# Attention: projection in 64-row halves beside the scores and exponents of the other half, attended values between such stretches

## The chip, the cores and the metric

The kernel runs on one core of a Trainium2 chip. The metric is device time in microseconds of one execution, the median of three runs. The core's engines work side by side, each through its own queue in order: TensorE (PE, with its weight loads listed as PEld), VectorE (DVE), ScalarE (ACT), GpSimd (POOL), and SyncE (SP), which only issues DMAs. TensorE multiplies on an array of 128 by 128 cells; a matmul that uses only 64 rows of its operands takes one half of the array, rows 0 to 63 or rows 64 to 127, and one that writes 32 partitions takes a column strip. Its results land in PSUM, eight banks of 512 numbers a partition, where VectorE and ScalarE read them.

## The reference

Two pairs of layers on x of 2048 tokens by 576 features. Each pair is windowed attention and then a spectral filter, both behind a layer norm and added to x:

```python
def _A_ref(x, wqkv, wo):            # H = 32 heads of 18, window W = 256
    q, k, v = (x @ wqkv), by head
    scores = einsum("bhqd,bhkd->bhqk", q, k) * 18 ** -0.5
    scores = where(0 <= q_index - k_index < 256, scores, -1e9)
    o = einsum("bhqk,bhkd->bhqd", softmax(scores), v)
    return o @ wo
def _B_ref(x, w_r, w_i):
    return irfft2(rfft2(x) * (w_r + 1j * w_i))
x = x + _A_ref(layernorm(x)); x = x + _B_ref(layernorm(x))     # and both once more
```

## The kernel before, in words

The change touches the middle of each attention layer, the function `layer_a`, which is run once for each of the two attention layers.

The layer first makes xh and xl, the normalised x transposed and split into a high and a low part, and v. Then q and k are made by **projection**: `proj(i, c)` (L787) makes 128 rows of the joint q and k (block i of 9) for 512 tokens (c of 4) in a PSUM tile pj, as 14 matmuls of 128 rows that add up (high by high, low by high, high by low; `k_steps` gives the order). I call one (i, c) a *unit*. When its last matmul is issued, ScalarE copies the high part of the tile to sg (L813), and a `remainder` is noted: VectorE makes the low part (L816) and a DMA stores both to qk_d (L818). `remainders()` runs what is noted. At the eighth matmul of c = 2 the weights of block i + 1 are split (L796).

The heads go in 8 groups of four. `stack_load` brings a group's rows from qk_d into the tiles qs and ks: two heads in rows 0 to 63 and two in rows 64 to 127, each as high and low slots stacked, so that one matmul of 64 rows gives a whole score. The two heads of a half are told apart by `pair`, the halves by `hp`.

A group has 16 blocks of 128 tokens, and x counts blocks over all groups, 0 to 127. For a block there are three things to do:

- `score_max(x, pair, hp)` (L844): a matmul S of 63 rows gives the scores of 128 queries against up to 384 keys, and VectorE takes their masked maximum (L859). After four blocks `m_rows` turns the maxima with a transpose tpm, ScalarE negates them to mt, and a DMA writes them to the 64th row of qs.
- `exps(x, pair, hp)` (L877): a matmul E of 64 rows gives the transposed scores less the maximum, and ScalarE writes their exponent to a tile P (L890). After the fourth one GpSimd clears what lies outside the window (L892, L895).
- `pv(x)` (L900): the attended values, eight matmuls with fp32 operands that add into the PSUM tile U. Four heads write four strips of 32 partitions. After four blocks ScalarE copies U to us (L914), and `norm` turns us with four transposes tpo and divides on VectorE.

The main loop (L955) counts a step t from -10 to 129. A step has scores for block t + 10, exponents for block t, attended values for block t - 2 and some matmuls of the projection. Its order on TensorE is: E of both halves, S of both halves, U, then E of both halves and S of both halves for the other pair, then the projection's matmuls, then at most one transposition (tpm or tpo) that is due. The matmuls of E come in pairs, rows 0 to 63 and then rows 64 to 127, and so do those of S. `goal` (L946 to L950) spreads the 22 units that remain at t = 2 over t = 2 to 102; a step in which a unit ends makes no transposition.

PSUM's eight banks: three for S (tpm and tpo too), three for E, one for pj, one for U. In the first units pj uses an E bank every other time; in the last steps half of the E use S banks.

The order on each engine is the order of the calls: nothing is rescheduled. After the loop come the output projection and the spectral filter, which the change touches only in the names of the banks they use first.

Of the kernel before, what the change touches and what calls it, by code (L numbers as in the profile page):

```python
# [8 lines left out]
F32 = mybir.dt.float32  # L9
# [6 lines left out]
S, D = 2048, 576  # L16
# [592 lines left out]
def layer_a(tc, ident, eps, bp, src, dst, wqk_d, wv_d, wo_d, dc_d, gc_d, dram, copy, wvs, second, spectral, share):  # L609
# [17 lines left out]
    if True:  # L627
# [134 lines left out]
        with ExitStack() as c2:  # L762
# [24 lines left out]
            def proj(i, c, bank=0):  # L787

                box = {}
                ks = k_steps()  # L790
                cs = slice(c * 512, c * 512 + 512)

                def mm(s, k):
                    wk, p, xk = k
                    if s == 7 and c == 2 and 0 < i < 8:
                        w_split(i + 1)  # L796
                    if s == 0:
                        box["ps"] = pp.tile([128, 512], F32, tag="E" if bank else "pj", name=f"pj{i}_{c}", bufs=3 if bank else 1)
                    w = wt[i][0] if p == "h" else wt[i][1]
                    x = tokens(xT(xk, slice(0, S)), c) if second else xT(xk, cs)  # L800
                    T.matmul(box["ps"].rearrange("r (n p) -> r n p", n=NT) if second else box["ps"], w[:, wk], x, start=s == 0, stop=s == len(ks) - 1)  # L801
                    if s == len(ks) - 1:
# [17 lines left out]
                return [lambda s=s, k=k: mm(s, k) for s, k in enumerate(ks)]  # L820
# [25 lines left out]
            def score_max(x, pair, hp):  # L846
# [4 lines left out]
                if t == hp == pair == 0:  # L851
                    ms[n, c] = wp.tile([128, 2, 2, 4], F32, tag="m", name=f"m{n}_{c}", bufs=3)
# [9 lines left out]
            def m_rows(n, c):  # L862
                q = qs[n % 2]
                tp = pp.tile([128, 4, 128], F32, tag="S" if t >= 0 else "E", name=f"tpm{n}_{c}", bufs=3)
# [10 lines left out]
            pt = {}  # L875

            def exps(x, pair, hp):  # L877
# [5 lines left out]
                if hp == pair == 0:  # L883
# [3 lines left out]
                ps = pp.tile([128, 512], F32, name=f"E{x}_{hl_}", **(dict(tag="S", bufs=3) if pair and NX - LEAD <= x < NX - 4 else dict(tag="E", bufs=3)))  # L887
# [3 lines left out]
                if hp == pair == 1:  # L891
# [39 lines left out]
            for k, (i, c) in enumerate(((0, 0), (1, 0), (0, 1), (1, 1), (0, 2), (0, 3), (1, 2), (1, 3))):  # L931
                for f in proj(i, c, k % 2):
                    f()
# [9 lines left out]
            pj = [f for i in range(2, 9) for c in range(4) for f in proj(i, c, c % 2 if i == 2 else c == 0 and i == 3)]  # L943
# [11 lines left out]
            for t in range(-LEAD, NX + 2):  # L955
# [29 lines left out]
                for f in more:  # L985
                    f()
                if t >= 1:
                    remainders()
# [109 lines left out]
```

## Time and profile before

| | |
|---|---|
| three runs | 1567.22, 1568.28, 1578.97 us, median 1568.28 |
| span of the profiled execution, first to last instruction | 1561.3 us |
| the median less that span | 7.0 us |
| TensorE busy | 1495.4 us, 96% of the span |
| weight loads | 1086.4 us, 70% |
| VectorE, ScalarE, GpSimd busy | 976.1, 806.4, 624.6 us |
| mean granted TensorE clock | 0.993 |

The page gives a span for the profiled execution and no other time of its own, so the 7.0 us are taken against the median. In a line of the profile the first word after the numbers is the engine, L801 is line 801 of the kernel, `pj<-xh,wqh` is the output and the inputs, `64*128 64x384` a matmul's weights and its moving operand. Ends of matmuls are modelled; starts are measured. In a row of the chain or of the waits the name behind the arrow is what ended the wait.

### The profile page before, as it was taken

To read this page: it belongs to the slowest core of one execution; us is meant where nothing else is said; L and a number is where in the kernel's file an instruction comes from. 1 tells how busy PE (TensorE), PEld (TensorE's weight loads), DVE (VectorE), ACT (ScalarE), POOL (GpSimd) and SP (SyncE) were. 2 spreads that over 40 slices of the span, in tenths; PEclk is the share of its full clock that TensorE was granted. 3 is DMA by queue.
4 is the path that set the end of the run, shared out by engine and by line. 5 is a ranking of instruction groups with operands and counts; after the bars stand their busy time and mean duration, and the time that the engine had idled before them with its cause. 6 is when DMAs were issued, how large, how long until landed. Compare 5 with 4: busy or idle time off the path is not lost.

```text
span 1561.3 us, 34502 instructions
## 1 busy us (share of the span) xinstructions
PE 1495.4 (96%) x12124; PEld 1086.4 (70%) x12124; DVE 976.1 (63%) x3152; ACT 806.4 (52%) x1900; POOL 624.6 (40%) x1026
## 2 busy tenths in 40 slices
PE   7999999999999899999999999999999998999998
PEld 7975555555555899858999755555555558998598
DVE  4327777777775555455852377777777755554577
ACT  5523666666667344323454246666666673442243
POOL 2172444444446233162321823443443563322434
PEclk9999999999999999999999999999999999999999
DMA  6656455555553456666764564555535543657664
GB/s 196 186 178 213 138 163 175 155 157 171 153 162 99 144 181 193 214 240 226 257 166 96 184 209 136 151 149 148 144 122 144 150 142 116 199 183 248 213 217 137
DMA packets 203130, 267.62 MB, mean 171 GB/s; under 512 B 103183, under 2 KB 108303, under 8 KB 201999
## 3 DMA queue, kind: packets, MB, share of 16 engines
q1 hardware_dynamic: 194638, 245.44, 51.8%
q10 hardware_dynamic: 7680, 15.59, 2.8%
q0 software_dynamic: 640, 4.39, 1.0%
q8 instruction: 97, 1.59, 0.4%
q14 instruction: 75, 0.61, 0.1%
HBM read 166.71 MB, written 102.00 MB: 172 GB/s over the span
## 4 chain that ended last, share of the span: by engine, by line
PE 70%; DVE 7%; DMA 6%; ACT 5%; POOL 5%; issue 1%; SPq 1%; POOLq 0%; DVEq 0%; ACTq 0%
PE pj L801 16%; PE U L909 11%; PE E L889 11%; PE S L857 7%; PE ops L555 6%; PE vps L738 4%; PE pf L202 3%; PE pz L215 3%; DMA ofree<-yd 2%; PE pi L361 2%; PE tpo L919 2%; ACT P L890 2%; PE po L382 2%; DVE ofree L298 1%; POOL uv L302 1%
## 5 line engine op out<-in xcount | busy, mean ns | idle before, releaser
L859 DVE CUSTOM_DVE_ANT_0 jk<-S,mask 128x384 bf16<-128x384 f32 (+2 forms) x1024 | 499.0, 529 | 148.8 <-PE S L857 146.0
L890 ACT ACTIVATE P<-E 128x384 f32<-128x384 f32 (+2 forms) x1024 | 423.2, 474 | 200.6 <-PE E L889 185.3
L892 POOL TENSOR_SCALAR_AFFINE_SELECT P<-P 128x512 f32<-128x512 f32 x256 | 163.0, 637 | 440.1 <-ACT P L890 438.0
L889 PE MATMUL E<-qs,ks 64*128 64x384 f32 (+2 forms) x1024 | 235.6, 429 | 12.4 <-ACT P L890 9.0
L857 PE MATMUL S<-ks,qs 63*128 63x384 f32 (+2 forms) x1024 | 212.3, 351 | 3.2 <-DVE m L859 2.4
L909 PE MATMUL U<-P,vq 128*19 128x128 f32 (+1 forms) x3840 | 204.9, 332 | 1.0 <-POOL P L895 1.0
L889 PEld LDWEIGHTS E<-qs,ks 64*128 64x128 f32 x1024 | 103.7, 184 | 145.3 <-ACT P L890 81.7
L909 PEld LDWEIGHTS U<-P,vq 128*19 128x19 f32 x3840 | 90.5, 98 | 101.3 <-issue 36.3
L801 PE MATMUL pj<-xh,wqh 128*128 128x512 f32 x360 | 158.0, 439 | 2.1 <-ACT vt L742 1.7
L895 POOL TENSOR_SCALAR_AFFINE_SELECT P<-P 128x512 f32<-128x512 f32 x224 | 142.6, 636 | 0.0
L857 PEld LDWEIGHTS S<-ks,qs 63*128 63x128 f32 x1024 | 116.5, 188 | 37.2 <-DVE m L859 27.1
L555 PE MATMUL ops<-oroom 128*128 128x288 f32 x840 | 120.8, 299 | 4.4 <-DVE oroom L538 3.0
L801 PE MATMUL pj<-xh,wql 128*128 128x512 f32 x360 | 122.9, 414 | 0.1
L801 PE MATMUL pj<-xl,wqh 128*128 128x512 f32 x288 | 120.9, 420 | 0.0
L555 PEld LDWEIGHTS ops<-oroom 128*128 128x128 f32 x840 | 112.8, 189 | 6.2 <-DVE oroom L538 4.0
L801 PEld LDWEIGHTS pj<-xh,wqh 128*128 128x128 f32 x360 | 68.0, 189 | 37.3 <-issue 24.2
L816 DVE TENSOR_TENSOR sg<-pj,sg 128x512 fp32r<-128x512 f32 x72 | 49.8, 691 | 61.8 <-ACT sg L813 61.8
L171 POOL TENSOR_TENSOR eo<-xn 128x287 f32<-128x287 f32 x32 | 26.1, 817 | 153.1 <-ACT xn L169 142.1
L859 DVE DVE_READ_ACCUMULATOR2_ANT m<- 128x1 f32 x1024 | 85.2, 83 | 0.0
L813 ACT CAST sg<-pj 128x512 fp32r<-128x512 f32 x72 | 42.4, 588 | 75.4 <-PE pj L801 73.8
L361 PE MATMUL pi<-oroom 128*128 128x256 f32 (+1 forms) x576 | 76.0, 285 | 5.4 <-ACT oroom L346 4.0
L801 PEld LDWEIGHTS pj<-xh,wql 128*128 128x128 f32 x360 | 64.7, 188 | 23.5 <-issue 13.5
(177 smaller groups left out, 2593.7 us busy)
## 6 DMA issues: line engine op xcount, KB each, us to landing
qk_d<-sg SPq DMA_DIRECT2D x56, 512.0 KB
qs<-qk_d SPq DMA_DIRECT2D x384, 72.0 KB
ks<-qk_d SPq DMA_DIRECT2D x384, 72.0 KB
v_d<-vt SPq DMA_DIRECT2D x32, 304.0 KB
vq<-v_d SPq DMA_DIRECT2D x16, 608.0 KB
yd<-ye SPq DMA_DIRECT2D x32, 290.0 KB
wt<-in_w SPq DMA_DIRECT2D x16, 580.0 KB
x<-ofree SPq DMA_DIRECT2D x32, 288.0 KB
```

What stands on the lines that cost most here:

```text
L361: T.matmul(o, z[:, sl, c, lo:lo + m], mo, start=k == 0, stop=k == 5)
L555: self.nc.tensor.matmul(self.ps[u][n][:, 0:288], x, self.w[p][:, wk * D + n * 288:wk * D + n * 288 + 288], start=first and i == 0, stop=la ...
L738: T.matmul(ps[:, n, 0:288], xT(xk, c), w[:, wk, n * 288:(n + 1) * 288], start=i == 0, stop=i == len(ks) - 1)
L801: T.matmul(box["ps"].rearrange("r (n p) -> r n p", n=NT) if second else box["ps"], w[:, wk], x, start=s == 0, stop=s == len(ks) - 1)
L816: V.tensor_sub(rest[:, 1], by, rest[:, 0].bitcast(F32))
L857: T.matmul(ps[:, 0:N], q[b:b + 63, pair, i * 128:i * 128 + 128], k[b:b + 63, pair, lo:hi], start=True, stop=True)
L859: V.tensor_tensor_reduce(out=jk[:, 0:N], in0=ps[:, 0:N], in1=mask[:, 384 - N:384], scale=1.0, scalar=-3e38, op0=ALU.add, op1=ALU.max, accu ...
L889: T.matmul(ps[:, 0:nq], k[b:b + 64, pair, j * 128:j * 128 + 128], q[b:b + 64, pair, j * 128:j * 128 + nq], start=True, stop=True)
L890: A.activation(p[:, hl_, 0:nq], ps[:, 0:nq], AF.Exp, scale=SC)
L892: P.affine_select(out=p[:, :, 0:128], in_=p[:, :, 0:128], pattern=[[0, 4], [1, 128]], compare_op=ALU.is_ge, fill=0.0, base=0, channel_mult ...
L895: P.affine_select(out=p[:, :, 256:384], in_=p[:, :, 256:384], pattern=[[0, 4], [-1, 128]], compare_op=ALU.is_gt, fill=0.0, base=0, channel ...
L909: T.matmul(U[32 * h:32 * h + 19, (q0 % 4) * 128:(q0 % 4) * 128 + 128 * (q1 - q0)], vts[n][:, j, h], pt[n, j][:, h, (q0 - j) * 128:(q1 - j) ...
```

## The change

The projection matmuls of the 22 units after t = 2 are cut into halves of 64 rows: a unit is 14 matmuls on the lower rows and 13 on the upper (the last product of low by low is left out), 27 in place of 14. They go beside E and S of the other half of the array.

A step of t = 2 to 102 becomes: `half` on one side, a drain of TensorE, `pv`, the transposition that is due, `half` on the other side. A `half` has four matmuls of one half of the array (E for two pairs, S for two pairs) and two or three projection matmuls of the other half, merged by a running sum of 176 for an E or S and 230 for a projection matmul. The side alternates so that the second `half` of a step and the first of the next are on the same side; in the first `half` of a step (at = 0) the order is S, E, S, E, in the second (at = 1) E, S, E, S.

The lower and the upper matmuls of a unit add to the same bank, at different times. The banks change: two for E (three before), two for pj (one before). From t = 103 the old order stays, and the second pair of E uses the banks of pj. A step in which a unit ends now makes its transposition as well. Which of the four exponents of a block comes first now varies, so the tiles P and m are made at the first and the masks at the fourth, whichever it is. The first six of the remaining units and the eight before them stay whole, all on the two pj banks.

```diff
-            def proj(i, c, bank=0):
+            def proj(i, c):
-                box = {}
-                ks = k_steps()
+                box = dict(n=0)
...
-                def mm(s, k):
+                def mm(r, k, of, cue):
                     wk, p, xk = k
-                    if s == 7 and c == 2 and 0 < i < 8:
+                    if cue and c == 2 and 0 < i < 8:
                         w_split(i + 1)
-                    if s == 0:
-                        box["ps"] = pp.tile([128, 512], F32, tag="E" if bank else "pj", name=f"pj{i}_{c}", bufs=3 if bank else 1)
+                    if box["n"] == 0:
+                        box["ps"] = pp.tile([128, 512], F32, tag="pj", name=f"pj{i}_{c}", bufs=2)
+                    box["n"] += 1
...
-                return [lambda s=s, k=k: mm(s, k) for s, k in enumerate(ks)]
+                ks = k_steps()
+                whole = [lambda s=s, k=k: mm(slice(0, 128), k, 14, s == 7) for s, k in enumerate(ks)]
+                lower = [lambda s=s, k=k: mm(slice(0, 64), k, 27, s == 7) for s, k in enumerate(ks)]
+                upper = [lambda k=k: mm(slice(64, 128), k, 27, False) for k in ks[:13]]
+                return whole, lower, upper
...
-                ps = pp.tile([128, 512], F32, name=f"E{x}_{hl_}", **(dict(tag="S", bufs=3) if pair and NX - LEAD <= x < NX - 4 else dict(tag="E", bufs=3)))
+                tag = "E" if x < MIX or not pair else "S" if NX - LEAD <= x < NX - 4 else "pj"
+                ps = pp.tile([128, 512], F32, name=f"E{x}_{hl_}", tag=tag, bufs=3 if tag == "S" else 2)
...
-            for m in range(22):
-                a, b = [2 + 23 * z // 5 for z in (m, m + 1)]
-                for t in range(a, b):
-                    goal[t] = 84 + 14 * m - (-14 * (t + 1 - a) // (b - a))
+            MIX = 103
+            units = [proj(i, c) for i in range(2, 9) for c in range(4)]
+            pj = [f for u in units[:6] for f in u[0]]
+            halves = [[f for u in units[6:] for f in u[side]] for side in (1, 2)]
+            def half(t, hp, at):
+                side = halves[1 - hp]
+                k = len(side) - (22 * (14 - 1 + hp)) * (MIX - 1 - t) // (MIX - 2)
+                steps = [(230 * z, z, f) for z, f in enumerate(side[:k])]
+                del side[:k]
+                ops = [(exps, t, 0), (score_max, t + LEAD, 0), (exps, t, 1), (score_max, t + LEAD, 1)]
+                if not at:
+                    ops = [ops[z] for z in (1, 0, 3, 2)]
+                steps += [(176 * z + 1, z, lambda f=f, x=x, pair=pair: f(x, pair, hp)) for z, (f, x, pair) in enumerate(ops)]
+                for _, _, f in sorted(steps, key=lambda z: z[:2]):
+                    f()
+                remainders()
...
+                mix = 2 <= t < MIX
...
+                if mix:
+                    half(t, 1 - t % 2, 0)
+                    T.drain()
+                    if 0 <= t - 2 < NX:
+                        pv(t - 2)
-                for pair in range(2):
+                for pair in range(0 if mix else 2):
...
                 for f, n, c in [] if ends and t >= 2 else due[:1]:
                     f(n, c)
                     due.pop(0)
+                if mix:
+                    half(t, t % 2, 1)
```

More of the change, by code (lines that the diff above doesn't have):

```diff
@@ L850, in score_max @@
                 q, k = qs[n % 2], ks_[n % 2]
-                if t == hp == pair == 0:
+                if (n, c) not in ms:
                     ms[n, c] = wp.tile([128, 2, 2, 4], F32, tag="m", name=f"m{n}_{c}", bufs=3)
@@ L873, in m_rows @@
                                           mt[r:r + 4].bitcast(F32))
-            pt = {}
+            pt, made = {}, {}
             def exps(x, pair, hp):
@@ L984, in layer_a @@
                         more = more[(len(more) + 1) // 2:]
[L985 to L988, printed above, removed]
+                if not mix:
+                    for f in more:
+                        f()
+                    if t >= 1:
+                        remainders()
                 if copy and t >= 32 and t % 4 == 0 and t < 32 + 16 * len(copy):
```

26 lines of the change are left out of this document (13 added, 13 removed).

## The prediction, made before the change was run

> **What bounds the kernel now.** I read the page from its busy shares to the chain that ended last, then cut out the stage that the change touches, then looked at one of its steps instruction by instruction.
>
> ```profile
> span 1561.3 us, 34502 instructions
> ...
> PE 1495.4 (96%) x12124; PEld 1086.4 (70%) x12124; DVE 976.1 (63%) x3152; ACT 806.4 (52%) x1900; POOL 624.6 (40%) x1026
> ...
> PE 70%; DVE 7%; DMA 6%; ACT 5%; POOL 5%; issue 1%; SPq 1%; POOLq 0%; DVEq 0%; ACTq 0%
> PE pj L801 16%; PE U L909 11%; PE E L889 11%; PE S L857 7%; PE ops L555 6%; PE vps L738 4%; PE pf L202 3%; PE pz L215 3%; DMA ofree<-yd 2%; PE pi L361 2%; PE tpo L919 2%; ACT P L890 2%; PE po L382 2%; DVE ofree L298 1%; POOL uv L302 1%
> ```
>
> TensorE is on 70% of the chain, and the four kinds of matmul that the change rearranges (projection pj, attended values U, exponent inputs E, scores S) hold 45% of the span. The table by stages, between the attended values of step 1 and of step 101 in each layer:
>
> ```profile
> 148.32:447.34 299.02, 295.78 (x2731) 165.15 (x2729) 223.66 (x869) 197.12 (x476) 129.75 (x208) 1.00 0.53 158
> 925.21:1224.69 299.48, 296.33 (x2731) 164.71 (x2729) 223.66 (x869) 197.21 (x476) 122.05 (x192) 1.00 0.50 143
> ```
>
> A hundred steps take 299 us, so one takes 2.99, in both layers and at a granted clock of 1.00 (the figure behind the five engines). The engines stand in the order TensorE, weight loads, VectorE, ScalarE, GpSimd: VectorE has 224 of the 299 us, ScalarE 197. So TensorE sets the step, and the next engine is a quarter below it. Inside a step, from the timeline (start, length as modelled; only the starts are used here):
>
> ```profile
> 312.92 0.45 PE L889 MATMUL E<-qs,ks 64*128 64x384 f32 x2
> 313.20 0.34 PE L857 MATMUL S<-ks,qs 63*128 63x384 f32 x2
> 313.47 0.85 PE L909 MATMUL U<-P,vq 128*19 128x256 f32 x16
> 314.25 0.44 PE L889 MATMUL E<-qs,ks 64*128 64x384 f32 x2
> 314.52 0.34 PE L857 MATMUL S<-ks,qs 63*128 63x384 f32 x2
> 314.80 0.50 PE L801 MATMUL pj<-xh,wqh 128*128 128x512 f32 x1
> 315.13 0.39 PE L801 MATMUL pj<-xl,wqh 128*128 128x512 f32 x1
> 315.36 0.40 PE L801 MATMUL pj<-xh,wqh 128*128 128x512 f32 x1
> 315.60 0.27 PE L865 MATMUL tpm<-ident,m 128*16 128x128 f32 x1
> 315.80 0.45 PE L889 MATMUL E<-qs,ks 64*128 64x384 f32 x2
> ...
> 318.72 0.60 PE L919 MATMUL tpo<-ident,us 128*128 128x128 f32 x4
> 319.25 0.45 PE L889 MATMUL E<-qs,ks 64*128 64x384 f32 x2
> ```
>
> What the reader should see: a pair of E or S, one matmul on each half of the array, starts together and costs the time of one; and every change of array layout costs. From pj to the next pj is 0.23, but the first pj after S needs 0.33: 0.10 is a weight load that nothing covers. E to S is 0.28, of which again about 0.10 is load, so a 384-wide pair streams in 0.17. S to pj or U is 0.27, which leaves 0.10 for the changeover itself. So a changeover costs 0.10, and 0.20 where full-width weights follow. A step has four: into U (0.10), out of U (0.20), into pj (0.20), out of pj (0.20), together 0.70. Streams: four pairs 0.68, U 0.78 less the 0.10 of its way out, 0.68, and 3.05 pj (22 units of 14 over 101 steps) at 0.23, 0.70. With the transposes (tpo 0.53 less the 0.10 changeover that pj would have had, once in four steps; tpm 0.10 net, once in four) 0.13. Sum 2.89; the other 0.10 is waiting.
>
> **The change part by part.** It acts on 101 steps a layer, 202 in all.
>
> Streams: nothing. A step after has eight E and S on one half, 8 x 0.17 = 1.36, beside 27 x 22 / 101 = 5.88 half-height pj on the other, 5.88 x 0.23 = 1.35. Before it was 0.68 + 0.70 = 1.38. The same columns pass; they are only paired otherwise.
>
> Does a pair out of step run as fast as one in step? The trace has a few such places, where one half had waited:
>
> ```profile
> 476.54 0.44 PE L889 MATMUL E<-qs,ks 64*128 64x384 f32 x1 [0.38 <-ACT P L890]
> 476.64 0.54 PE L857 MATMUL S<-ks,qs 63*128 63x384 f32 x2
> ...
> 485.59 0.34 PE L857 MATMUL S<-ks,qs 63*128 63x384 f32 x2
> 485.60 0.19 PEld L889 LDWEIGHTS E<-qs,ks 64*128 64x128 f32 x1
> 485.77 0.33 PE L889 MATMUL E<-qs,ks 64*128 64x384 f32 x1
> ```
>
> At 476.64 two S of the two halves overlap though they start 0.20 apart (0.54 for both, 0.34 for one), and at 485.60 a half loads its next weights while it streams: the next matmul starts after 0.18. So I take the halves as independent.
>
> Changeovers: into and out of pj go, **-0.40**. But the transposes lose their place beside pj: they now stand behind U, with a changeover and load of their own, 0.20, in two steps of four, **+0.10**.
>
> The drain: 202 of them, ahead of U. No row shows one in the middle of a kernel. It must wait until results have landed. E at 314.25 streams until 314.53, and its reader starts at 314.72:
>
> ```profile
> 314.72 0.87 ACT L890 ACTIVATE P<-E 128x384 f32<-128x384 f32 x2 [0.46 <-PE E L889]
> ...
> 485.79 0.87 ACT L890 ACTIVATE P<-E 128x384 f32<-128x384 f32 x2 [1.30 <-PE E L889]
> 486.33 0.18 PEld L889 LDWEIGHTS E<-qs,ks 64*128 64x128 f32 x1 [0.55 <-ACT P L890]
> ...
> L890 ACT ACTIVATE P<-E 128x384 f32<-128x384 f32 x352 | 153.2, 492 | 70.9 <-PE E L889 63.6 <-PE S L857 4.2 <-PE U L909 1.7
> ```
>
> That is 0.20, an estimate of the emptying. Restarting costs 0.05: the ACT that began at 485.79 ends 0.49 later, at 486.28, and the waiting load starts at 486.33. So 0.25 in place of the 0.10 of an ordinary changeover: **+0.15**. Below: nothing, if the changeover already empties the array. Above: the waits table has idle of U's weight loads put down to issue, at most 0.4 long.
>
> ```profile
> PEld E L889 <- ACT P L890: 32.5, 100, 0.7
> ...
> PEld U L909 <- issue: 13.9, 58, 0.4
> ```
>
> A drain with such a gap behind it costs 0.20 + 0.40 - 0.10 = 0.50. I take 0.15, the nearer row being that of a wait of this very stage. Behind the drain stand U's sixteen matmuls, a transpose and the next stretch; ACT and VectorE wait for that stretch, and have 1.0 and 0.7 us of a step to spare.
>
> The banks: E has two in place of three, pj two in place of one. Between two U a stretch now brings E S E S | S E S E on one half. By hand, from the start of the first load at 0: E1 streams 0.10 to 0.27, S1, then E2 0.44 to 0.61; unhindered, E3 would stream from 0.95 and E4 from 1.29, ending at 1.46. ACT reads E1 from 0.27 + 0.20 = 0.47 to 0.96, and its bank is free at 1.01. E3's load waits for that on TensorE's queue, with the pj steps behind it; E3 streams from 1.11, 0.16 late. ACT starts a second exponent 0.38 after the first (0.87 for the two), so E2's bank is free at 0.85 + 0.49 + 0.05 = 1.39. E4's load waits for it and streams from 1.49 to 1.66: the stretch is 0.20 longer. VectorE reads a score in 0.56:
>
> ```profile
> 300.40 0.56 DVE L859 CUSTOM_DVE_ANT_0 jk<-S,mask 128x384 bf16<-128x384 f32 x1 [0.17 <-PE S L857]
> ```
>
> It reads S1, streamed by 0.44, from 0.64 to 1.20, and its bank (one of three, as before) is free at 1.25, about when S4 loads; four reads and the little else that it has leave it at 2.24 a step. So **+0.20**, with nothing at the lower end, if ACT takes the exponents sooner than I reckon, and 0.34 at the upper, the second rival's.
>
> Other edits. The projection's stores, weight splits (same step, same unit) and loads keep their steps: a unit ends within a step of where it did, a head group's rows are loaded some four steps or more after the last unit they need, and scored ten steps later. Nothing on SP's or POOL's queue moves past anything that is late. POOL finishes a step's probabilities one step ahead of U. In the steps after 103 the second pair of E gets pj's two banks, four in all instead of three; the wait there is
>
> ```profile
> PEld E L889 <- ACT P L890: 8.5, 23, 0.7
> ```
>
> 8.5 us in layer 1, and I give back a quarter of it, 2 us a layer, -4.
>
> Sum per step: -0.40 + 0.10 + 0.15 + 0.20 = +0.05, and x 202 = +10; less 4, **+6 us**. Span 1561.3 becomes 1567. The runs' median, 1568.28, is 7.0 above the span of the profiled execution; the same lies around it after, so 1574.
>
> **The rivals.**
>
> Faster: *the drain is free.* If the 0.10 changeover is already an emptying of the array, the drain adds nothing: 1574 - 202 x 0.15 = 1544. For it: U's first load today follows the last S only after that gap. Against it: a reader needs 0.20, not 0.10, after the stream ends, and a drain waits like a reader.
>
> Slower: *ACT's other work falls into the stretch.* With two E banks every ScalarE instruction between E1 and E4 delays both halves at once, since they share one queue. By the same window,
>
> ```profile
> L914 ACT COPY us<-U 128x512 f32<-128x512 f32 x25 | 14.7, 587 | 1.2
> ...
> L813 ACT CAST sg<-pj 128x512 fp32r<-128x512 f32 x22 | 13.0, 590 | 2.4 <-PE pj L801 2.3
> ```
>
> they are 27.7 us per 100 steps, 0.28 a step; if half of it delays an exponent, +0.14 x 202 = +28: 1602. It decides from the point where they come behind E1 instead of beside U. The copy of U comes before E1 and should fit; the cast comes at any place of the stretch.
>
> Slower too: *one weight load at a time.* If a half can't load while the other does, the 14 loads of a stretch follow one another. At 0.10 to 0.11 each, as read from the starts, they take 1.40 to 1.54, where the streams take 1.36; I take +0.11, x 202 = +22: 1596. It decides from 1.36 / 14 = 0.097 for a load. Against it: a pair's two loads cost the 0.10 of one.
>
> *Matmuls must end in order.* A 384-wide E issued right behind a 512-wide pj would have to end 0.06 after its own time; the lane catches up within the stretch, so about +0.05 a step, +10: 1584. The trace has only pairs of equal width and can't tell. The Trainium skill (TensorE: Matmul & The Clock Gate, Part 3, "What overlaps and what doesn't") states that matmuls start and end in program order; by it this rival is the one that holds. The same place says that a weight load overlaps a running matmul only on other rows of the array; the row at 485.60 shows it on the same rows, and the measurement decides.
>
> *It doesn't do what it says:* halves of different kinds run one after the other. Then 1.36 + 1.35 in place of 1.36, +1.35 x 202 = +273: about 1850. Against it: the rows of 476.64.
>
> **How the numbers follow.** Forecast 1574: 0.40. Drain free, 1544: 0.25. ACT's other work, 1602: 0.18. One load at a time, 1596: 0.06. Ends in order, 1584: 0.07. Not side by side, 1850: 0.04. The forecast's own spread is some 15 us, from the bank wait (0.13 to 0.27 a step). Half of the first rival, with a shorter bank wait, lies below 1544, down to 1534 for most; the slow ones reach 1612 if ACT delays a little more than half: 1534 to 1612 leaves out the 1850, the dear drain (1574 + 202 x 0.35 = 1645, for which only the longest of 58 waits speaks) and the tails. A measurement of this kernel tells about 1% from no change, 15.7 us. Faster by over 1% (below 1553): most of the drain rival and a little of the forecast, 0.26. Slower (above 1584): the two slow mechanisms, half of the ends in order, the 1850, and the forecast's upper edge, 0.36. Within: 0.38.
>
> **What would show it.** In the profile after: E and pj starting together in the timeline, E to S 0.17 apart in a stretch; no 0.33 for a first pj; 0.25 between the end of a stretch and U's first load (0.10 if the drain is free, more than 0.3 if it is dear); the row of E's weight loads waiting for ACT at some 20 us more per 100 steps; VectorE's 224 us unchanged, at the same share of a step of 3.0 us. The prediction is wrong if the step is under 2.93 or over 3.07 us, and its reason is wrong if the drain and the banks don't carry it.

## The result, and the profile after

The changed kernel takes 1580.45 us (median of 20 runs, 1576.78 to 1586.00), the kernel before took 1570.75 us beside it (20 runs, 1562.67 to 1578.97). The ratio is 1.0063, with a 95% interval of 1.0047 to 1.0079: the change costs about 0.6%. The forecast was 1574. From profile to profile the span grew from 1561.3 to 1576.3 us, by 15.0, where 6 were forecast. The medians lie closer than the spans because of the clock: both profiled executions had a mean granted clock of 0.993, but the 52 executions of the kernel before that stand beside the experiments have 0.988 by median, and the 20 of the changed kernel 0.9925. Those with 0.992 or more take 1564.4 us (8 of the kernel before) and 1579.6 us (17 of the changed kernel) by median, so that at a like clock the change costs 15 us, 1.0%. Four lines of the page of the changed kernel answer to those shown of before (span, busy shares, and the chain by engine and by line):

```profile
span 1576.3 us, 35829 instructions
...
PE 1483.9 (94%) x12696; PEld 1127.6 (72%) x12696; DVE 964.6 (61%) x3152; ACT 810.6 (51%) x1900; POOL 622.8 (40%) x1026
...
PE 70%; DVE 7%; ACT 6%; DMA 4%; POOL 3%; issue 3%; SPq 1%; POOLq 0%; DVEq 0%; ACTq 0%
PE pj L801 15%; PE U L916 12%; PE E L895 7%; PE S L862 7%; PE ops L555 6%; PE vps L738 4%; PE pf L202 3%; PE pz L215 3%; PE tpo L926 2%; ACT P L896 2%; PE pi L361 2%; PE po L382 2%; ACT sg L813 1%; DMA yd<-ze 1%; PE pq L313 1%
```

TensorE still holds 70% of the chain, and its four kinds of matmul 41% of the span in place of 45%. What is new is "issue": 3% in place of 1%, time in which the engine waited for nothing that the profile shows. The same hundred steps, from the attended values of step 1 to those of step 101, in the table by stages of the changed kernel (length, then TensorE, weight loads, VectorE, ScalarE, GpSimd, granted clock):

```profile
146.88:453.91 307.03, 290.76 (x3010) 183.46 (x3010) 218.45 (x870) 200.00 (x479) 130.28 (x210) 1.00 0.52 157
931.17:1239.33 308.16, 291.97 (x3009) 183.98 (x3009) 218.02 (x868) 199.99 (x478) 122.07 (x193) 1.00 0.50 142
```

A step takes 3.070 and 3.082 us where it took 2.990 and 2.995: 8.0 and 8.7 us more per hundred, 16.7 in all, which is more than the 15.0 of the span (in the 25 steps behind them 61.9 and 59.3 us became 58.2 each, 4.8 us back; elsewhere 3.1 are lost). TensorE's busy time within a step fell, and VectorE and ScalarE have what they had. So TensorE waits where it did not wait before. One usual step of the changed kernel, in the timeline:

```profile
347.09 0.85 PE L916 MATMUL U<-P,vq 128*19 128x256 f32 x16
347.86 0.49 PE L801 MATMUL pj<-xl,wqh 64*128 64x512 f32 x1
347.87 0.44 PE L895 MATMUL E<-qs,ks 64*128 64x384 f32 x1
348.15 0.34 PE L862 MATMUL S<-ks,qs 63*128 63x384 f32 x1
348.20 0.39 PE L801 MATMUL pj<-xh,wqh 64*128 64x512 f32 x1
348.33 0.34 PE L895 MATMUL E<-qs,ks 64*128 64x384 f32 x1
348.43 0.39 PE L801 MATMUL pj<-xl,wqh 64*128 64x512 f32 x1
348.50 0.33 PE L862 MATMUL S<-ks,qs 63*128 63x384 f32 x1
348.66 0.39 PE L801 MATMUL pj<-xh,wql 64*128 64x512 f32 x1
348.68 0.33 PE L862 MATMUL S<-ks,qs 63*128 63x384 f32 x1
348.97 0.44 PE L895 MATMUL E<-qs,ks 64*128 64x384 f32 x1
348.98 0.49 PE L801 MATMUL pj<-xh,wql 64*128 64x512 f32 x1
349.25 0.34 PE L862 MATMUL S<-ks,qs 63*128 63x384 f32 x1
349.31 0.39 PE L801 MATMUL pj<-xh,wql 64*128 64x512 f32 x1
349.43 0.36 PE L895 MATMUL E<-qs,ks 64*128 64x384 f32 x1
349.90 0.41 PE L916 MATMUL U<-P,vq 128*19 128x256 f32 x4
```

The reader should see four things. The two halves do run beside each other: pj and E start at 347.86 and 347.87. Each starts at its own pace, pj every 0.23, E and S every 0.18, and the start of an S does not wait for the longer pj beside it. At 348.97 the third E comes 0.29 after S instead of 0.18, and the S behind it another 0.28 after that instead of 0.18. And from the last E to U pass 0.47 us, with the drain, where before 0.27 passed from S to U. From U to U this step has 2.81 us; steps of this kind in the kernel before, with three pj in them, had 2.77.

Two rows of the table of waits, of the same hundred steps of layer 1 of the changed kernel (us in total, times, longest):

```profile
PEld U L916 <- issue: 33.2, 91, 0.5
PEld E L895 <- ACT P L896: 30.1, 83, 1.0
```

The idle time of U's weight loads for nothing that the profile shows grew from 13.9 to 33.2; E's wait for ScalarE did not grow in sum: 32.5 before. It moved. Of the 32.5, 24.8 stood at the first E behind a pj (49 times) or behind U (33 times), where the layout of the array changes; of the 30.1, 22.3 stand at the third E of a stretch (64 times). The row counts all idle time of the weight loads, also what passes under a running stream.

### The profile page after: what moved, and what is told of

It reads as the page before. It is cut to its first block, busy times and chain, and to the rows that moved or that the text cites. A ratio compares the mean times of both kernels' runs of the same rounds, so it can differ in the third digit from the quotient of the medians.

```text
span 1576.3 us, 35829 instructions
## 1 busy us (share of the span) xinstructions
PE 1483.9 (94%) x12696; PEld 1127.6 (72%) x12696; DVE 964.6 (61%) x3152; ACT 810.6 (51%) x1900; POOL 622.8 (40%) x1026
## 4 chain that ended last, share of the span: by engine, by line
PE 70%; DVE 7%; ACT 6%; DMA 4%; POOL 3%; issue 3%; SPq 1%; POOLq 0%; DVEq 0%; ACTq 0%
PE pj L801 15%; PE U L916 12%; PE E L895 7%; PE S L862 7%; PE ops L555 6%; PE vps L738 4%; PE pf L202 3%; PE pz L215 3%; PE tpo L926 2%; ACT P L896 2%; PE pi L361 2%; PE po L382 2%; ACT sg L813 1%; DMA yd<-ze 1%; PE pq L313 1%
## 5 line engine op out<-in xcount | busy, mean ns | idle before, releaser
L895 PE MATMUL E<-qs,ks 64*128 64x384 f32 (+2 forms) x1024 | 353.4, 387 | 13.5 <-ACT P L896 8.5
L862 PE MATMUL S<-ks,qs 63*128 63x384 f32 (+2 forms) x1024 | 299.8, 348 | 6.6 <-DVE m L864 5.8
L801 PE MATMUL pj<-xh,wqh 64*128 64x512 f32 (+1 forms) x580 | 242.5, 427 | 2.4 <-ACT vt L742 1.7
L895 PEld LDWEIGHTS E<-qs,ks 64*128 64x128 f32 x1024 | 172.4, 184 | 92.0 <-ACT P L896 69.5
L862 PEld LDWEIGHTS S<-ks,qs 63*128 63x128 f32 x1024 | 174.1, 186 | 45.7 <-DVE m L864 23.7
L801 PE MATMUL pj<-xl,wqh 64*128 64x512 f32 (+1 forms) x464 | 197.8, 426 | 0.0
L801 PE MATMUL pj<-xh,wql 64*128 64x512 f32 (+1 forms) x536 | 184.3, 424 | 0.1
L801 PEld LDWEIGHTS pj<-xh,wqh 64*128 64x128 f32 (+1 forms) x580 | 106.7, 185 | 27.0 <-issue 15.9
L801 PEld LDWEIGHTS pj<-xh,wql 64*128 64x128 f32 (+1 forms) x536 | 93.4, 185 | 19.5 <-issue 12.2
L801 PEld LDWEIGHTS pj<-xl,wqh 64*128 64x128 f32 (+1 forms) x464 | 86.0, 185 | 15.7 <-issue 10.0
```

The lines of the kernel that those rows point to most:

```text
L862: T.matmul(ps[:, 0:N], q[b:b + 63, pair, i * 128:i * 128 + 128], k[b:b + 63, pair, lo:hi], start=True, stop=True)
L895: T.matmul(ps[:, 0:nq], k[b:b + 64, pair, j * 128:j * 128 + 128], q[b:b + 64, pair, j * 128:j * 128 + nq], start=True, stop=True)
```

## Experiments

Five questions were put to the chip: what the drain costs, whether E's two banks make the stretch wait, what the last steps owe to four banks, what ScalarE's other work costs, and whether the halves beside each other are free. Each run has its own runs of the kernel before beside it, 1568 to 1573 us by median.

### The drain

The drain orders the two halves of the rows, which add into one bank of the projection. Taken away alone, nothing would order them; that was not tried. In its place a read can order them: ScalarE reads one column of the bank that is still open behind the last pj of the first stretch, and the first pj of the second stretch waits for that read. (In this kernel each projection matmul also ends its own group, `stop=True`, so that the bank may be read in between.)

```diff
 def half(t, hp, at):
     ...
     for at_, z, f in sorted(steps, key=lambda z: z[:2]):
         f()
+        if not at and (at_, z) == last:
+            for ps in seen.values():
+                A.copy(wp.tile([128, 1], F32, tag="see", ...), ps[:, 0:1])
...
                     half(t, 1 - t % 2, 0)
-                    T.drain()
```

> TensorE's drain between the first stretch and the attended values is gone; in its place ScalarE reads one column of the open projection bank (128x1) behind the stretch's last projection matmul, and the second stretch's first projection matmul waits for that read, which ends while the attended values run. Theory 1 (the drain itself is paid: in the trace of the changed kernel 0.46 us pass from the last E's start to U's start with it, 0.27 passed from S to U without one before): 0.19 less in each of 202 steps, the step of layer 1 goes from 3.07 to 2.88 us, the whole from 1580 to about 1542 us, and U's wait for nothing the profile shows shrinks from 33 us per 100 steps to about 14. Theory 2 (the array must be empty before U's weights go in anyway, the drain only shows it): step 3.07 and 1580 us, within 0.5%. Theory 3 (the new read of some 0.2 us in ScalarE's queue makes E's banks come later by as much as the drain cost): about 3.07 as well, but E's wait for ScalarE grows by 15 us or more per 100 steps while U's shrinks.

It takes 1546.24 us, 0.9826 of the kernel before (0.9787 to 0.9866), 34 us less than the changed kernel and 1.7% less than the kernel before. Its hundred steps of layer 1 in the table by stages, the end of its step in the timeline, and U's wait:

```profile
148.44:439.19 290.75, 283.87 (x3012) 181.44 (x3010) 218.47 (x870) 206.83 (x593) 130.14 (x209) 1.00 0.54 165
```

```profile
340.40 0.34 PE L900 MATMUL E<-qs,ks 64*128 64x384 f32 x1
...
340.67 0.14 PEld L921 LDWEIGHTS U<-P,vq 128*19 128x19 f32 x8 [0.18 <-issue]
340.67 0.41 PE L921 MATMUL U<-P,vq 128*19 128x256 f32 x4
340.85 0.15 ACT L980 COPY see<-pj 128x1 f32<-128x1 f32 x1
```

```profile
PEld U L921 <- issue: 16.1, 79, 0.3
```

The step is 2.907 us, 0.163 less than with the drain, E to U is 0.27 again, and U's wait is back at 16.1 us per hundred steps. The read itself takes 0.15 us and ends, at 341.00, while U runs.

Two controls go with it. One keeps the drain and has the reads as well.

> The reads of the run before, with the drain left in: the price of the reads alone. If they are hidden, step 3.07 us and 1580 us within 0.5%; if ScalarE's queue is what E waits for, up to 0.2 us more in each of 202 steps, up to 1620 us.

It takes 1577.93 us (1.0026, 0.9998 to 1.0054), 3.068 us a step: the reads are free, and the difference of 31.7 us between these two kernels is the drain's alone, 0.157 for each of 202. The other control has a second drain.

```diff
                 if mix:
+                    T.drain()
                     half(t, t % 2, 1)
```

> A second drain of TensorE in each mixed step, behind the attended values and the transposes. Theory 1 (a drain costs the end of the running stream and the load that could have lain under it, whatever comes next): 0.10 to 0.19 us more in each of 202 steps, 1600 to 1618 us. Theory 2 (a drain is free where the array's row use changes anyway, as it does between U and the stretch): 1580 us within 0.5%.

It takes 1610.90 us (1.0244, 1.0193 to 1.0294), 3.229 us a step: 0.159 more for the second drain, about as much as for the first. The wait now stands at the first weight load behind it as well (pj's row had 14.7 in the changed kernel), as the table of waits of this kernel shows for the same hundred steps:

```profile
PEld pj L801 <- issue: 35.4, 100, 0.4
PEld U L916 <- issue: 33.1, 91, 0.5
```

So a drain is not free where the layout changes anyway, and it costs about the same ahead of U and ahead of the stretch. A drain where the layout stays was not run.

### The banks

First the order of the scores and exponents, with the number of banks kept.

```diff
     ops = [(exps, t, 0), (score_max, t + LEAD, 0), (exps, t, 1), (score_max, t + LEAD, 1)]
-    if not at:
-        ops = [ops[z] for z in (1, 0, 3, 2)]
```

> Both stretches of a step run E S E S, instead of S E S E in the first and E S E S in the second: two E's then stand 0.18 us apart where the stretches of two steps meet less often, and the first E of a stretch finds its bank earlier or later. By two banks, ScalarE's 0.388 us per exponent and its start 0.20 us behind the stream, E's fourth bank comes free 0.17 us later than now: about 0.17 more per step, 1614 us, if two banks are what the step waits for. If the banks never limit, 1580 us within 0.5%.

It takes 1611.07 us (1.0232, 1.0185 to 1.0278), 3.213 us a step, 0.143 more, where 0.17 was worked out; E's wait for ScalarE rose from 30.1 to 43.1 us:

```profile
PEld E L895 <- ACT P L896: 43.1, 104, 1.0
```

So the stretch is sensitive to when a bank comes free. The other three runs asked which bank. Two of them made the whole projection ahead of the mixed steps, so that its banks were free for E.

```diff
-            pj = [f for u in units[:6] for f in u[0]]
-            halves = [[f for u in units[6:] for f in u[side]] for side in (1, 2)]
+            pj = [f for u in units for f in u[0]]
+            halves = [[], []]
...
+            goal[1] = len(pj)
...
-                k = len(side) - (22 * (14 - 1 + hp)) * (MIX - 1 - t) // (MIX - 2)
+                k = 0
```

> The changed kernel with the 22 units made whole ahead of the mixed steps, which then hold only E, S, the drain, U and the transposes; E keeps two banks. It puts 22 x 14 streams of 0.227 us = 70 us of TensorE in front, in each layer. Theory 1 (a half of the projection beside the other side's scores costs the step nothing of its own): the step of layer 1 stays at 3.0 to 3.07 us and the whole is about 140 us longer, 1705 to 1720 us. Theory 2 (the halves share the array, and half of the projection's stream is paid): 3.05 x 0.227 = 0.69 less per step, about 2.4 us, and the whole stays near 1580 us.

```diff
-                tag = "E" if x < MIX or not pair else "S" if NX - LEAD <= x < NX - 4 else "pj"
+                tag = "E" if not pair else "S" if NX - LEAD <= x < NX - 4 else "pj"
```

> The run before, with the projection's two banks, which stand empty in these steps, given to E: four banks in place of two. Theory 1 (two banks make E wait for ScalarE): 0.20 us less per step than the run before, about 40 us less in all. Theory 2 (the wait that the profile puts down to ScalarE is only the engines' pace): the same step and time as the run before.

They took 1969.69 us (1904 to 1984) and 1926.81 us (1852 to 2000), far over what either theory gave, for a reason that has a part of its own below: the granted clock fell to 0.50 in most of the mixed steps. Only stretches at 1.00 can be compared, a few steps in each run. There the usual step, from U to U, has 2.77 us with two banks and 2.78 with four. The times of the two runs, whose ranges overlap, tell nothing of the theories. By the steps at 1.00 the first theory of the first run holds (the halves cost the step next to nothing), and of the second run the step of the second theory: four banks for E gain nothing. Its reason, the engines' pace, does not follow from that. Where the time goes instead, the timeline of the run with four banks shows (TensorE, and below it VectorE):

```profile
508.97 0.33 PE L895 MATMUL E<-qs,ks 64*128 64x384 f32 x1
509.26 0.44 PE L862 MATMUL S<-ks,qs 63*128 63x384 f32 x1
509.54 0.34 PE L895 MATMUL E<-qs,ks 64*128 64x384 f32 x1
509.99 0.41 PE L916 MATMUL U<-P,vq 128*19 128x256 f32 x4
```

```profile
508.64 0.56 DVE L864 CUSTOM_DVE_ANT_0 jk<-S,mask 128x384 bf16<-128x384 f32 x1 [0.77 <-PE S L862]
509.12 0.08 DVE L864 DVE_READ_ACCUMULATOR2_ANT m<- 128x1 f32 x1
```

The third E doesn't wait any more, but the last S does: it starts at 509.26, 0.29 after E, when VectorE's read of the first S, which is done at 509.12 to 509.20, gives back the bank (S has three). The E behind it follows after 0.28. The step loses as much as it lost to E's bank. In the step of the changed kernel shown first, S's bank stands as close: VectorE's read of the first S ends at 349.08, and the weight load of the S of 349.25 starts at 349.14. This reading was put to the test with readers that hold no bank long: VectorE's maximum over 128 scores, and ScalarE's exponent over 128 columns, the rest left out.

```diff
-                V.tensor_tensor_reduce(out=jk[:, 0:N], in0=ps[:, 0:N], in1=mask[:, 384 - N:384], ...)
+                M = 128 if 2 <= x - LEAD < MIX else N
+                V.tensor_tensor_reduce(out=jk[:, 0:M], in0=ps[:, N - M:N], in1=mask[:, 384 - M:384], ...)
```

> The changed kernel, with the row maximum taken over 128 of the up to 384 scores in the mixed steps (the rest is left out): VectorE holds a bank of S some 0.3 us less. Theory 1 (E's two banks and ScalarE alone make the stretch wait): the usual step stays at 2.81 us, the whole at 1580. Theory 2 (S's three banks and VectorE alone): 0.21 less per step, 1538 us. Theory 3 (both queues come free at about the same time, so that each covers the other): 0.03 to 0.06 less per step, 1568 to 1574 us.

```diff
+                    if 2 <= x < MIX and nq > 128:
+                        V.memset(pt[n, j][:, :, 128:nq], 0.0)
...
-                A.activation(p[:, hl_, 0:nq], ps[:, 0:nq], AF.Exp, scale=SC)
+                m = 128 if 2 <= x < MIX else nq
+                A.activation(p[:, hl_, 0:m], ps[:, 0:m], AF.Exp, scale=SC)
```

> The run before, and the exponents too taken over 128 of the 384 columns, the rest set to zero by VectorE: no bank is held long by either reader. Theory 3 of the run before: the stretch's waits go altogether, 0.15 to 0.21 less per step than the changed kernel, 1538 to 1550 us. If the stretch is paced by TensorE itself (streams, loads and the drain), 1580 us as in the changed kernel.

With the maximum alone shortened the kernel takes 1576.54 us (1.0056, 1.0032 to 1.0079) and 3.052 us a step; the usual step stays at 2.81, though VectorE's busy time per hundred steps fell from 218 to 141 us. With both shortened it takes 1547.76 us (0.9864, 0.9821 to 0.9907) and 2.907 us a step, and the usual one 2.58. First the third E and its neighbours with the maximum shortened, then with both:

```profile
348.13 0.51 PE L862 MATMUL S<-ks,qs 63*128 63x384 f32 x2
...
348.61 0.44 PE L896 MATMUL E<-qs,ks 64*128 64x384 f32 x1
```

```profile
338.49 0.33 PE L862 MATMUL S<-ks,qs 63*128 63x384 f32 x1
338.66 0.35 PE L898 MATMUL E<-qs,ks 64*128 64x384 f32 x1
...
338.85 0.34 PE L862 MATMUL S<-ks,qs 63*128 63x384 f32 x1
```

In the first the E still comes late, 0.30 after the second of the two S (348.31); in the second it comes after 0.17, and the S behind it after 0.19. So the two queues cover each other: free E's banks and S's hold the stretch (the run with four banks), free S's and E's hold it (the maximum shortened), free both and 0.23 us of the step go. The maximum alone gave what the first theory of that expectation said, a usual step of 2.81; only with the other two runs does the third theory hold, and its gain for the maximum alone, 0.03 to 0.06, came out as 0.018. That E's banks alone gain nothing was measured without the projection; the exponents alone were not shortened in the changed kernel.

### The last steps

```diff
-                tag = "E" if x < MIX or not pair else "S" if NX - LEAD <= x < NX - 4 else "pj"
+                tag = "E" if x < MIX or not pair else "S" if NX - LEAD <= x < NX - 4 else "E"
```

> The changed kernel, with E in the steps behind the projection's end kept to two banks. If four banks are what made those steps shorter than before (58.2 us against 61.9 and 59.3 for 25 steps), they go back to 60 to 64 us, and the whole is 3 to 11 us longer, 1583 to 1591 us. If the shorter stretch comes from elsewhere (other work that fell in it), nothing changes.

It takes 1589.92 us (1.0106, 1.0064 to 1.0147), and the 25 steps behind the mixed ones 61.5 us in each layer in place of 58.2. E's wait for ScalarE in these steps of layer 1, first in the changed kernel, then with two banks:

```profile
PEld E L895 <- ACT P L896: 3.3, 17, 0.2
```

```profile
PEld E L895 <- ACT P L896: 13.5, 40, 0.9
```

Here four banks do carry the gain, 3.3 us in each layer. It is less than the 10.2 us by which E's wait shrinks: with four banks S's weight loads wait 5.9 us for VectorE, with two 0.6, so S's third bank stands behind E's here too.

### ScalarE's other work, and a better order

Two runs tried to better the kernel with the read. One puts S first in both stretches.

> The kernel with the read in place of the drain, with S ahead of E in both stretches (S E S E | S E S E). By the banks worked out by hand (release 0.05 us behind the reader's end, ScalarE 0.39 us and VectorE 0.49 us for each, a reader's start 0.20 us behind its stream) the last E of a step starts 1.53 us into the two stretches, against 1.56 in the order E S E S | S E S E: 0.03 less per step, about 1540 us. If only the number of banks decides and not the order, 1546 us; if the E that comes 0.28 us later starts ScalarE's chain later and nothing is won back, 0.1 to 0.2 more per step, 1566 to 1586 us.

It takes 1563.33 us (0.9943, 0.9921 to 0.9966), 2.996 us a step: 0.09 more where 0.03 less was worked out. The timeline shows where it goes (TensorE, and its weight loads):

```profile
346.71 0.33 PE L867 MATMUL S<-ks,qs 63*128 63x384 f32 x1
...
347.10 0.44 PE L900 MATMUL E<-qs,ks 64*128 64x384 f32 x1
...
347.38 0.34 PE L867 MATMUL S<-ks,qs 63*128 63x384 f32 x1
```

```profile
347.10 0.18 PEld L900 LDWEIGHTS E<-qs,ks 64*128 64x128 f32 x1 [0.37 <-ACT P L901]
```

A wait for a bank costs the wait and a load. It is E's weight load that waits for ScalarE: it and its E both start at 347.10, 0.39 after S, so that nothing covers the load, and the S behind starts 0.28 after E in place of 0.18, as at the start of a stretch. In the step of the changed kernel shown first it is the same at 348.97 and 349.25. The last E of this run's step starts 1.66 into the two stretches (345.90 to 347.56), 0.13 after the 1.53 worked out by hand. The terms that the expectation lists hold no load; whether its 0.10 is what was left out isn't known.

The other issues the copy of a finished unit behind the last exponent ahead of U; until then the copy stood right behind the unit's last pj.

```diff
-                        A.copy(rest[:, 0], by)
+                        if of == 14:
+                            A.copy(rest[:, 0], by)
...
                         def remainder():
+                            if of == 27:
+                                A.copy(rest[:, 0], by)
                             V.tensor_sub(rest[:, 1], by, rest[:, 0].bitcast(F32))
...
-                remainders()
+                if not at:
+                    remainders()
```

> The kernel with the read in place of the drain; the copy of a finished projection unit (ScalarE, 128x512, about 0.5 us) is issued behind the last exponent of the stretch that ends at the attended values, and not in the middle of a stretch. In the trace of the kernel with the read, most of the steps in which such a copy falls into a stretch take 3.1 us and more where like steps without one take 2.61 (3.09 to 2.61, 22 units in each layer, some 14 of them in a stretch), and those where it falls 2.0 us or more into the step take 2.61. Theory 1 (the copy stands in ScalarE's queue ahead of exponents and holds E's banks): 14 x 0.45 = 6 us less per layer, 1534 us, down to 1526 if every unit's end costs it. Theory 2 (VectorE's subtraction for the unit, which comes as late as before or later, is what the stretch waits for): 1546 us, or a few more.

It takes 1547.07 us (0.9857, 0.9830 to 0.9885), the same as without the edit; its steps fell by 0.014 and 0.018 in the two layers. The step with the copy is short now (2.61 where it had 3.09), but the next one is longer by 0.2 to 0.4. The first theory has the gain wrong: it seems that the copy and the subtraction behind it delay the exponents and maxima of whatever stretch they precede. So the read in place of the drain, with or without this edit, is the fastest version found.

### The halves beside each other, and the clock

The run with the projection ahead tells what the halves cost: at a clock of 1.00 its usual step has 2.77 us, the changed kernel's 2.81, both with the waits for banks. A half of the projection beside a half of scores costs 0.04 us a step, and not 0.69. But without it the clock did not last. Three rows of that run's table by stages, with two banks for E: the first mixed steps, the rest of them, and the steps behind them.

```profile
223.33:260.00 36.67, 34.97 (x319) 22.18 (x319) 24.46 (x104) 23.10 (x55) 14.59 (x24) 1.00 0.34 101
270.00:640.00 370.00, 361.38 (x1962) 244.11 (x1962) 175.61 (x686) 168.18 (x362) 100.12 (x168) 0.50 0.27 77
660.00:700.00 40.00, 37.33 (x412) 20.66 (x400) 30.49 (x120) 31.36 (x81) 25.35 (x37) 1.00 0.29 79
```

The same loop runs at 1.00 for some 40 us and then at 0.50 for 370, with matmuls in flight for 361 of the 370. Behind it stand steps without any projection too, with E and S of both sides beside each other, and there the clock is 1.00. One more run gave that order to the mixed steps.

```diff
-                mix = 2 <= t < MIX
+                mix = False
...
                     if pair == 0 and 0 <= t - 2 < NX:
+                        if 2 <= t < MIX:
+                            T.drain()
                         pv(t - 2)
```

> The run with the projection ahead (two banks for E, drain kept), with the same matmuls in another order: the scores and exponents of the two sides stand beside each other (E E S S of one pair, drain, U, E E S S of the other), where that run did one side in each stretch with the other half of the rows empty. There the granted clock was 0.50 in most of the mixed steps and 1.00 in the steps behind them, which have both sides beside each other. Theory 1 (what decides is how much of the array's rows work at once): the clock stays at 0.95 to 1.00, a step takes 2.3 to 2.6 us, the whole 1590 to 1660 us. Theory 2 (what decides is the amount of work in a step once the projection is gone): the clock falls to 0.50 here too, a step takes 3.5 us or more and the whole 1800 us or more.

It takes 1741.51 us (1.1075, 1.1000 to 1.1149):

```profile
218.56:532.96 314.40, 274.99 (x2426) 141.93 (x2426) 212.57 (x849) 183.73 (x451) 122.46 (x205) 0.90 0.39 111
```

The mean clock is 0.90 in this layer and 0.85 in the other, in place of 0.55: better, and neither theory's number; the step at 1.00 is 2.90 us and not 2.3 to 2.6, likely because two E of one pair now ask for both banks at once (E's weight loads wait 69.2 us per hundred steps for ScalarE, against 30.1 in the changed kernel). Rows side by side help to hold the clock; what it goes by exactly stays open.

## Why the prediction was right and wrong

The sum said +0.05 us a step, and the chip +0.08 and +0.09; the last steps were to give back 4 us and gave 4.8. That the forecast of 1574 came within 7 us of 1580.45 is in part luck: it put 7.0 us on the span for the median, and the changed kernel's median stands only 4.1 above its span, so that in spans, at a like clock, the miss is 9 us. Point by point:

**Streams, nothing.** Right. The halves start out of step as well as in step, each at its own pace; beside scores the projection's half costs 0.04 us a step.

**Changeovers, -0.40.** No run does it alone. By an estimate from three: a usual step had 2.77 before; with neither bank waits nor drain it would have 2.58 less 0.20 (2.81 with the drain, 2.61 without), 2.38, so -0.39. Right, with one detail wrong: the first pj of a stretch still needs 0.34 (347.86 to 348.20), but E beside it has its own 0.28, so it costs nothing.

**Transposes, +0.10.** Right, by like steps of layer 1 that hold no end of a unit and don't follow one (medians). In the changed kernel a step with tpo has 3.47 us and its like without a transpose 2.82, 0.65 more; in the kernel before, with three pj, 3.15 and 2.76, 0.39 more. A tpm adds 0.21 (3.02) where it added 0.07 (2.83). One step in four each: about +0.10.

**The drain, +0.15.** Right: 0.157 by the two kernels that differ by it alone, 0.159 for a second one. The rival that it is free, which had 0.25 and would have made the change a gain of 24 us, falls; so does the upper bound of 0.50. The estimate from a reader's start (0.20) and a released load (0.05) was a good one. In a usual step U's load stands at 0.29 behind the end of the stretch (the E of 349.43, 0.17 long, to 349.89 by the trace), where 0.25 was said.

**Two banks for E, +0.20.** The size was right and the cause half wrong, and this is the step that failed. Freed of its readers, the usual step loses 0.23 and the mean step 0.163. But E's banks alone don't do it: with four of them the step stays, because S's third bank stands close behind. The prediction had that in its own working, "its bank is free at 1.25, about when S4 loads", and took it for no cost; it is the second half of the limit. It also had two late E in a stretch, and the trace of the usual step has one: its load starts at 348.97, 0.11 after the E itself would have started, and another 0.10 is that load, 0.21 together. The row that was to show "some 20 us more per 100 steps" shows 2.4 less, because the prediction took the 32.5 us of before for a floor: 24.8 of them stood at changeovers and went with these, and 22.3 came at the third E.

**ScalarE's other work (the rival with 0.18 at 1602).** It takes place, but that it carried the time past 1574 isn't shown. In layer 1 of the changed kernel, leaving out the first place of the sixteen, 16 steps are longer than the shortest of their place, by 7.6 us together, 0.08 a step; 12 of them have a unit's copy in them and are longer by 0.39 to 0.58. The kernel before paid as much, one step later. Of its 18 steps of layer 1 that directly follow a unit's end and have a like elsewhere (the same number of pj and the same transposes), 13 are longer by 0.39 or more, and the 18 by 7.2 us together. Two rows of such a step:

```profile
200.03 0.69 DVE L816 TENSOR_TENSOR sg<-pj,sg 128x512 fp32r<-128x512 f32 x1 [0.25 <-ACT sg L813]
...
201.24 0.18 PEld L857 LDWEIGHTS S<-ks,qs 63*128 63x128 f32 x1 [0.32 <-DVE m L859]
```

There VectorE's subtraction for the unit stood ahead of its maxima, and S waited for a bank. The prediction's sum of the step before has it, at most, within the 0.10 that it calls waiting.

**Ends in order (the rival with 0.07 at 1584).** The traces speak for it, at a small price. The first E behind U, with a pj issued just ahead of it, starts at 347.87 in the step shown first, and ScalarE's exponent at 348.43: 0.56 later, and 0.56 by median in 22 such places. Without a pj it is 0.48 (median of 5 in the run with the projection ahead, 6 in the one with four banks) and was 0.48 in the kernel before. First the changed kernel, then the run with the projection ahead:

```profile
348.43 0.87 ACT L896 ACTIVATE P<-E 128x384 f32<-128x384 f32 x2 [0.89 <-PE pj L801]
```

```profile
238.85 0.44 PE L895 MATMUL E<-qs,ks 64*128 64x384 f32 x1
...
239.33 0.87 ACT L896 ACTIVATE P<-E 128x384 f32<-128x384 f32 x2 [0.80 <-PE E L895]
```

The E of 348.97, whose pj is issued behind it, has its exponent 0.54 later, its like without a pj (239.88) 0.53. So an E's reader seems to wait for the longer pj ahead of it, some 0.08, where the rival had 0.06 at an end; starts are not held back. E's bank comes free that much later, and the third E waits for that bank, so that what it costs is part of the banks' term above; all that pj costs a usual step is 0.04, this included, where the rival had 0.05 on top.

**The other rivals.** One load at a time and not side by side fall with the timeline (both halves load while both stream, and the step is 3.07, not 4.3).

Together: -0.39 + 0.10 + 0.16 + 0.16 make +0.03, beside the measured 0.08; the first term is one of a usual step, the last two are means over all steps, and what the remaining 0.05 is stays open. In the usual step, which went from 2.77 to 2.81, the drain (0.20) and the banks (0.23) each cost more than was put down for them. The bound that the prediction set itself, a step of 2.93 to 3.07, was just met in layer 1 (3.070) and passed in layer 2 (3.082).

## What to carry to other kernels

When two reuses of buffers stand at nearly the same time, count both: freeing either alone shows next to nothing, and a wait costs the wait and then the load that it kept from being prepared. A wait in the profile before is no floor to add to: see first where it stands, and whether the change takes that place away. Look at what a barrier on an engine is there to order, and see whether a read by another engine, for next to nothing, can order it: here that turned a change that cost 0.6% into one that gains 1.7%. And when work is moved out of the way to price it, look at the granted clock before comparing any times.

## What the runs showed of the hardware

A drain of TensorE in the middle of a kernel costs 0.16 us in the mean, 0.20 in an undisturbed step, also where the layout changes. A weight load that had to wait for its bank is itself uncovered: 0.10 us more. Two 64-row halves with streams of 512 and 384 columns run beside each other at 0.23 and 0.18 us each; the reader of an E with a pj issued just ahead starts 0.56 us after that E, and 0.48 without.

The granted clock fell to 0.50 while matmuls were in flight for 361 of 370 us, when scores and exponents used one half of the rows with the other half empty, and it held at 1.00 in the hundred steps of the changed kernel, whose other half was busy. The Trainium skill (TensorE: Matmul & The Clock Gate, Part 1, "The HAM clock gate") says that the gate follows how busy TensorE has been, with half rate and full rate as its two states. The two values agree with the rows here; busy in the sense of a matmul being in flight does not, since the profile, which models the ends of matmuls, has 98% at the half rate.
